# Linear attention and an erf-gated MLP in split fp32: order of the gates' forms, of the product's chunks, and of the gates' halves

## The chip, the cores and the metric

The kernel runs on one core of a Trainium2 chip. The metric is the device time of one execution in microseconds, as the median of three runs. The profile is of one further execution. Engines are named as in the profile: PE is TensorE (PEld its weight loads), DVE is VectorE, ACT is ScalarE, SP is SyncE, which here only issues DMAs, and POOL is GpSimd.

## The reference

A linear attention (8 batches, 8 heads, 576 tokens, head size 64) is normalised per head and feeds a gated MLP over all 4608 tokens:

```
kv  = einsum('bhsd,bhse->bhde', k, v)
o   = einsum('bhsd,bhde->bhse', q, kv)
x   = o / sqrt(mean(o*o, -1) + 1e-6) * g_norm      # to (4608, 512)
h   = x @ w_in                                     # 512 -> 2048
g   = h * erf(softplus(h))
out = g @ w_out                                    # 2048 -> 512
```

## The kernel before

The tokens are worked on in nine tiles of 512. T = 0 to 7 hold the first 512 tokens of each batch; T = 8 (which the code calls B) collects the last 64 of all eight. The MLP's 2048 hidden features are cut into 16 blocks of 128, and four blocks make a batch (BATCH = 4), so a tile has four batches b = 0 to 3.

The order of the instructions on every engine is written by hand (manual_schedule): each engine runs its own instructions in program order, and the framework adds the semaphores for data and buffers. Buffers come from pools that rotate. The eight PSUM banks are two for attention (ps_at), and six that `product` rotates through, two to each product, so a product can start when what the third product before it left in the same banks has been read.

Tiles T = 0 and 1 are done first, with plain fp32 matmuls (lines 592 and 471), while the weights are read and split. From T = 2 on (after 268 us) all MLP matmuls are in a split form. Every operand exists in three forms: form 0, high (rounded on ScalarE by a scaled copy, `upper`, line 385), form 1, low (the rest, VectorE, line 388), and form 2, both (a combination, VectorE, line 389). `thirds` makes all three. The weights' forms wait in DRAM and are loaded tile by tile: w_in_parts for a hidden block, w_out_parts for an output block, 768 KB each. w_out_parts has seven buffers.

`product` multiplies two operands in forms: n_ps takes the sums of forms 0 and 1 over four chunks k (8 matmuls), m_ps the sum of form 2 (4 matmuls). For a hidden block the chunks are four groups of 128 of the 512 inputs, so chunk p of x_forms comes from head pair p. For an output row block j (128 of the tile's tokens) the chunks are the four feature blocks of the batch, each with its own w_out_parts tile.

The main loop runs over m, which counts batches across tiles; T and b belong to the hidden side of m, and the result side lags by one batch. One turn of the loop is:

- four hidden products, i = 0 to 3. After each, ScalarE copies n_ps, scaled, to h (line 717), VectorE adds m_ps (line 419, called `add`), and ScalarE takes softplus into s (line 719). At i = 0 and i = 1 the gates of the batch before, old_h, are cut into their three forms, one half of the tokens each (g_forms0, g_forms1), by `cut`.
- erf of s on ScalarE, in two instructions, with a table load ahead (line 724).
- four result products, j = 0 to 3, each added to the accumulator e by VectorE (line 665 or 414 for n_ps, line 419 for m_ps). With the last batch of a tile each j is followed by the store of its rows. After j = 1 VectorE multiplies h by s (line 735).
- between these, at numbered places, the pieces of attention for head pair b of the next tile: key-value products and transposes (lines 279 to 301), apply (306, 307), mean (328 to 342), norm (348, 351, 360) and split, which cuts the normalised x into x_forms. For the last tile T = 8, which is prepared during T = 7, the attention outputs already lie in x_last, and only square, mean, norm and split are left.
- loads of weights, put on SP's queue by `fetch` at fixed places.

After the last hidden batch (m = batches - 1) a final turn (m = batches) has results only; `g_next` hands it the half that was cut early.

The two lines that place the cut in the loop are:

```
            if len(g) <= i < 2:
                g.append(cut(old_h, i))
```

Of the kernel before, what the change touches and what calls it, by code (L numbers as in the profile page):

```python
# [43 lines left out]
AF = mybir.ActivationFunctionType  # L44
ALU = mybir.AluOpType
# [13 lines left out]
def kernel(  # L59
# [10 lines left out]
    nc = tc.nc  # L70
    P = 128
# [33 lines left out]
    def softplus_table():  # L105
        nc.scalar.preload_act_table_set("softplus")  # L106
# [34 lines left out]
    for i in range(2):  # L141
        nc.gpsimd.dma_start(
            out=g_col[i * D : i * D + D, :], in_=g_norm.rearrange("(d one) -> d one", one=1)
# [100 lines left out]
    def weights():  # L244

        w_next("split")
        w_next("join")
        w_next("load")
# [134 lines left out]
    def upper(x, high):  # L383

        nc.scalar.activation(high, x, AF.Copy, scale=1.0 + 2.0**-13)  # L385

    def lower(x, high, low, both):
        nc.vector.tensor_tensor(out=low, in0=x, in1=high.bitcast(FP32), op=ALU.subtract)  # L388
        nc.vector.scalar_tensor_tensor(  # L389
            out=both,  # L390
            in0=low.bitcast(FP32),
            scalar=SHIFT,
            in1=high.bitcast(FP32),
            op0=ALU.mult,
            op1=ALU.add,
        )

    def thirds(x, high, low, both):
        upper(x, high)
        lower(x, high, low, both)  # L400
# [17 lines left out]
    def add(out_, ps):  # L418
        nc.vector.tensor_tensor(out=out_, in0=ps, in1=out_, op=ALU.add)  # L419
# [3 lines left out]
    def product(weights, moving):  # L423

        n_ps, m_ps = (
            pool.tile([P, G], FP32, name=name, tag=tag)
            for name, (pool, tag) in zip(("n_ps", "m_ps"), banks[:2])
        )
        banks.extend(banks[:2])
        del banks[:2]  # L430
        for ps, forms in ((n_ps, (0, 1)), (m_ps, (2,))):
            for form in forms:
                for k in range(4):
                    nc.tensor.matmul(  # L434
                        ps,
                        lhsT=weights(form, k),
                        rhs=moving(form, k),
                        start=(form == forms[0] and k == 0),
                        stop=(form == forms[-1] and k == 3),
                    )  # L440
        return n_ps, m_ps
# [57 lines left out]
    def unit(name):  # L499
        return gate.tile([P, G], FP32, name=name, tag=name[0])  # L500
# [30 lines left out]
    first_batch, batches = FIRST * NB, NG * NB  # L531
# [6 lines left out]
    def load_parts(which, n):  # L538

        pool = w_in_p if which == "in" else w_out_p  # L540
        for _ in range(n):
            if w_seq[which]:
                key = w_seq[which].pop(0)
                t = pool.tile([P, 3, G], FP32, name=f"w_{which}_parts", tag="w")
                nc.sync.dma_start(out=t, in_=w_kept[key])
                w_now.setdefault(key, []).append(t)
# [22 lines left out]
    for n in range(FIRST * FC + 1):  # L569
# [16 lines left out]
        done = n - LAG + 1  # L586
        if 0 <= done < whole:
            nc.vector.tensor_tensor(out=hs[done], in0=hs[done], in1=ss[done], op=ALU.mult)
        if T < FIRST:
# [9 lines left out]
            if n == whole:  # L599
                old_h = wide.tile([P, BATCH, G], FP32, name="h", tag="h")  # L600
            h = hs[n] = old_h[:, n - whole] if n >= whole else unit("h_sb")
            s = ss[n] = unit("s_sb")
# [43 lines left out]
    def hidden(T, f):  # L646

        w = w_now["in", f].pop(0).rearrange("p i (c f) -> p i c f", c=KC).bitcast(FP32R)
        return product(lambda form, c: w[:, form, c], lambda form, c: x_forms[T][:, form, c])

    def cut(h, half):

        t = late_r.tile([P, 3, BATCH, 2 * P], FP32R, name=f"g_forms{half}")
        thirds(h[:, :, half * 2 * P : half * 2 * P + 2 * P], *(t[:, i] for i in range(3)))
        return t

    def result(T, b, j, g, w):

        ps = product(
            lambda form, f: g[j // 2][:, form, f, j % 2 * P : j % 2 * P + P],  # L660
            lambda form, f: w[f][:, form],
        )
        if b == 0:
            es[j] = acc.tile([P, DM], FP32, name="e", tag="e")
            nc.vector.tensor_scalar(
                out=es[j], in0=ps[0], scalar1=SHIFT - 1.0, scalar2=None, op0=ALU.mult
            )
        else:
            add_scaled(es[j], ps[0], SHIFT - 1.0)
        add(es[j], ps[1])  # L670
        if b == NB - 1:
            store(T, j, es.pop(j))
# [4 lines left out]
    g_next = []  # L677
    for m in range(first_batch, batches + 1):
        T, b = divmod(m, NB)
        todo = []  # L680
        if T + 1 < NG:
            todo = list(attention(T + 1, b))
            if b == 0:
                side = late_r if T % 2 == FIRST % 2 else late
                x_forms[T + 1] = side.tile([P, 3, KC, G], FP32R, name=f"x_forms{(T + 1) % 2}")

        def piece():
            if todo:
                todo.pop(0)()

        places = (0, 2, 3, 5, 7, 8)
        if T + 1 == B:
            places = (0, 0, 0, 5, 7, 7)
        elif T + 2 == B and b == NB - 1:
            places = (0, 2, 3, 5, 7, 7)

        def pieces(place):
            while todo and places[-len(todo)] <= place:
                todo.pop(0)()

        def fetch(place):
            for which in FETCH[place].split():
                load_parts(which, 1)

        pieces(0)
        g, g_next = g_next, []
        if m < batches:
            h = wide.tile([P, BATCH, G], FP32, name="h", tag="h")
            s = gate_r.tile([P, BATCH, G], FP32, name="s", tag="s")
        for i in range(BATCH):  # L710
            if m < batches:
                n_ps, m_ps = hidden(T, b * BATCH + i)
            fetch(i)
            if len(g) <= i < 2:
                g.append(cut(old_h, i))
            if m < batches:
                nc.scalar.activation(h[:, i], n_ps, AF.Copy, scale=SHIFT - 1.0)  # L717
                add(h[:, i], m_ps)
                nc.scalar.activation(s[:, i], h[:, i], AF.Softplus)  # L719
            pieces(i + 1)  # L720
        if m < batches:
            for i in range(2):
                part = s[:, 2 * i : 2 * i + 2]
                nc.scalar.activation(part, part, AF.Erf)  # L724
            if len(todo) < 3:
                softplus_table()
        T2, b2 = divmod(m - 1, NB)
        w = [w_now["out", b2 * BATCH + f].pop(0).bitcast(FP32R) for f in range(BATCH)]
        for j in range(J):
            result(T2, b2, j, g, w)  # L730
            fetch(BATCH + j)
            if j == 1 and m < batches:
                for i in range(2):
                    part = slice(2 * i, 2 * i + 2)
                    nc.vector.tensor_tensor(  # L735
                        out=h[:, part], in0=h[:, part], in1=s[:, part], op=ALU.mult
                    )
            if j == 2 and m == batches - 1:

                g_next.append(cut(h, 0))  # L740
            pieces(BATCH + 1 + j)
        old_h = h

# [32 lines left out]
```

## Time and profile before

| | |
|---|---|
| time, median of three runs | 981.02 us (979.07 to 981.49) |
| profiled execution | 979.31 us, span on the core 977.5 us, mean granted clock 0.997 |
| n_ps matmuls in `product`, 128x512 | 896 (hidden) and 928 (results) |
| m_ps matmuls in `product`, 128x512 | 448 and 464 |
| upper form of half the gates (ScalarE, 128x1024) | 58 times, 1055 ns |
| low form, both form of it (VectorE) | 58 times each, 1222 and 1225 ns |
| product of h and s (VectorE, 128x1024) | 56 times, 1218 ns |
| copy n_ps to h, softplus (ScalarE, 128x512) | 112 times each, 584 and 634 ns |

Busy shares and waits in the profile are to be read with one thing in mind: matmuls are pipelined, so each lasts about 0.39 us in the records but the next one starts 0.227 us after it. A product's twelve matmuls start within 2.72 us. A line of the timeline gives the start in us from the beginning of the span, the duration in us, the engine, the line and operation, the tiles written and read, and the count of instructions merged into it; in brackets stands the idle time ahead of it and who ended it.

### The profile page before, as it was taken

To read this page: it belongs to the slowest core of one execution; us is meant where nothing else is said; L and a number is where in the kernel's file an instruction comes from. 1 tells how busy PE (TensorE), PEld (TensorE's weight loads), DVE (VectorE), ACT (ScalarE), POOL (GpSimd) and SP (SyncE) were. 2 spreads that over 40 slices of the span, in tenths; PEclk is the share of its full clock that TensorE was granted. 3 is DMA by queue.
4 is the path that set the end of the run, shared out by engine and by line. 5 is a ranking of instruction groups with operands and counts; after the bars stand their busy time and mean duration, and the time that the engine had idled before them with its cause. 6 is when DMAs were issued, how large, how long until landed. Compare 5 with 4: busy or idle time off the path is not lost.

```text
span 977.5 us, 11728 instructions
## 1 busy us (share of the span) xinstructions
PE 944.5 (97%) x4328; PEld 677.0 (69%) x4328; DVE 728.8 (75%) x1031; ACT 615.9 (63%) x821; POOL 2.4 (0%) x10
## 2 busy tenths in 40 slices
PE   6899999999999999999999999999999999989997
PEld 4344444444478877787878777878787777768885
DVE  3987857865377777777777877777888777777666
ACT  4888765676666666666666666666666666665550
POOL 0000000000000000000000000000000000000000
PEclk9999999999999999999999999999999999999998
DMA  9865408879199886998599869987786669757952
GB/s 282 244 204 173 151 1 317 310 305 374 45 349 360 315 293 222 336 364 291 190 314 372 298 220 288 366 301 266 246 347 247 252 219 374 272 203 274 372 197 75
DMA packets 100936, 259.76 MB, mean 266 GB/s; under 512 B 44048, under 2 KB 57360, under 8 KB 100880
## 3 DMA queue, kind: packets, MB, share of 16 engines
q1 hardware_dynamic: 99248, 256.73, 73.7%
q10 hardware_dynamic: 1568, 2.29, 0.8%
q8 instruction: 34, 0.56, 0.2%
q14 instruction: 22, 0.18, 0.1%
q0 software_dynamic: 64, 0.00, 0.0%
HBM read 224.40 MB, written 34.60 MB: 265 GB/s over the span
## 4 chain that ended last, share of the span: by engine, by line
PE 75%; DVE 13%; ACT 7%; DMA 2%; issue 2%; SPq 0%; DVEq 0%
PE n_ps L434 33%; PE m_ps L434 17%; PE o_ps L471 9%; PE h_ps L592 8%; PE se_ps L307 3%; DVE h L735 3%; DVE e L419 2%; PE qt_ps L301 2%; PE kv_ps L279 1%; DVE x L360 1%; DVE h L419 1%; ACT s L719 1%; ACT s L724 1%; DVE e L414 1%; DMA v_sb<-in_v_dram 1%
## 5 line engine op out<-in xcount | busy, mean ns | idle before, releaser
L434 PE MATMUL n_ps<-x_forms,w_in_parts 128*128 128x512 f32 x896 | 233.0, 402 | 4.5 <-ACT x_forms L385 4.1
L434 PE MATMUL n_ps<-w_out_parts,g_forms 128*128 128x512 f32 x928 | 233.2, 393 | 4.0 <-DMA w_out_parts<-w_out 3.8
L434 PEld LDWEIGHTS n_ps<-w_out_parts,g_forms 128*128 128x128 f32 x928 | 174.4, 188 | 44.2 <-DMA w_out_parts<-w_out 5.1
L434 PEld LDWEIGHTS n_ps<-x_forms,w_in_parts 128*128 128x128 f32 x896 | 166.6, 188 | 48.3 <-issue 9.6
L719 ACT ACTIVATE s<-h 128x512 f32<-128x512 f32 x112 | 71.0, 634 | 203.7 <-DVE h L419 203.7
L434 PE MATMUL m_ps<-w_out_parts,g_forms 128*128 128x512 f32 x464 | 125.3, 392 | 1.1 <-DVE h L419 1.1
L434 PE MATMUL m_ps<-x_forms,w_in_parts 128*128 128x512 f32 x448 | 120.1, 390 | 0.0
L592 PE MATMUL h_ps<-xT,w_in_sb 128*128 128x512 f32 x256 | 115.0, 593 | 2.9 <-DVE xT L360 2.0
L419 DVE TENSOR_TENSOR h<-m_ps,h 128x512 f32<-128x512 f32 x112 | 77.0, 688 | 52.5 <-ACT h L717 49.7
L388 DVE TENSOR_TENSOR g_forms<-h,g_forms 128x1024 fp32r<-128x1024 f32 x58 | 70.9, 1222 | 46.9 <-ACT g_forms L385 46.6
L434 PEld LDWEIGHTS m_ps<-w_out_parts,g_forms 128*128 128x128 f32 x464 | 87.5, 189 | 20.2 <-DVE h L419 1.9
L471 PE MATMUL o_ps<-w_out_sb,h_sb 128*128 128x512 f32 x224 | 100.6, 592 | 0.0
L434 PEld LDWEIGHTS m_ps<-x_forms,w_in_parts 128*128 128x128 f32 x448 | 84.1, 188 | 17.7
L419 DVE TENSOR_TENSOR e<-m_ps,e 128x512 f32<-128x512 f32 x116 | 80.2, 692 | 16.7 <-PE m_ps L434 8.1
L592 PEld LDWEIGHTS h_ps<-xT,w_in_sb 128*128 128x128 f32 x256 | 48.4, 190 | 63.2 <-issue 56.9
L414 DVE SCALAR_TENSOR_TENSOR e<-n_ps,e 128x512 f32<-128x512 f32 x88 | 60.2, 684 | 24.6 <-PE n_ps L434 24.6
L471 PEld LDWEIGHTS o_ps<-w_out_sb,h_sb 128*128 128x128 f32 x224 | 42.1, 190 | 49.8 <-issue 48.0
L717 ACT ACTIVATE h<-n_ps 128x512 f32<-128x512 f32 x112 | 65.5, 584 | 15.0 <-PE n_ps L434 14.9
L389 DVE SCALAR_TENSOR_TENSOR g_forms<-g_forms 128x1024 fp32r<-128x1024 f32 x58 | 71.1, 1225 | 2.0
L735 DVE TENSOR_TENSOR h<-h,s 128x1024 f32<-128x1024 f32 x56 | 65.9, 1218 | 1.1 <-ACT s L724 1.1
L385 ACT ACTIVATE g_forms<-h 128x1024 fp32r<-128x1024 f32 x58 | 61.2, 1055 | 7.2 <-DVE h L735 5.7
L106 ACT ACT_TABLE_LOAD x44 | 56.5, 1283 | 0.8
(84 smaller groups left out, 940.4 us busy)
## 6 DMA issues: line engine op xcount, KB each, us to landing
w_out_parts<-w_out SPq DMA_DIRECT2D x116, 768.0 KB, 7.6
w_in_parts<-w_in SPq DMA_DIRECT2D x112, 768.0 KB, 6.3
w_in<-w_new SPq DMA_DIRECT2D x16, 768.0 KB, 5.6
w_out<-w_new SPq DMA_DIRECT2D x16, 768.0 KB, 6.5
k_sb<-in_k_dram SPq DMA_DIRECT2D x29, 288.0 KB, 5.6
v_sb<-in_v_dram SPq DMA_DIRECT2D x29, 288.0 KB, 5.5
q_sb<-in_q_dram SPq DMA_DIRECT2D x32, 256.0 KB, 5.4
w_raw<-in_moe_w_out_dram SPq DMA_DIRECT2D x8, 1024.0 KB, 5.1
```

The lines of the kernel that those rows point to most:

```text
L106: nc.scalar.preload_act_table_set("softplus")
L385: nc.scalar.activation(high, x, AF.Copy, scale=1.0 + 2.0**-13)
L388: nc.vector.tensor_tensor(out=low, in0=x, in1=high.bitcast(FP32), op=ALU.subtract)
L389: nc.vector.scalar_tensor_tensor(out=both, in0=low.bitcast(FP32), scalar=SHIFT, in1=high.bitcast(FP32), op0=ALU.mult, op1=ALU.add,)
L414: nc.vector.scalar_tensor_tensor(out=out_, in0=ps, scalar=scale, in1=out_, op0=ALU.mult, op1=ALU.add)
L419: nc.vector.tensor_tensor(out=out_, in0=ps, in1=out_, op=ALU.add)
L434: nc.tensor.matmul(ps, lhsT=weights(form, k), rhs=moving(form, k), start=(form == forms[0] and k == 0), stop=(form == forms[-1] and k == 3),)
L471: nc.tensor.matmul(o_ps[j], lhsT=g[:, j * P : j * P + P], rhs=w_out_sb[:, f, :], start=(f == 0), stop=last,)
L592: nc.tensor.matmul(h_ps, lhsT=w_in_sb[:, c, f * P : f * P + P], rhs=xT[T][:, c, :], start=(c == 0), stop=(c == KC - 1),)
L717: nc.scalar.activation(h[:, i], n_ps, AF.Copy, scale=SHIFT - 1.0)
L719: nc.scalar.activation(s[:, i], h[:, i], AF.Softplus)
L735: nc.vector.tensor_tensor(out=h[:, part], in0=h[:, part], in1=s[:, part], op=ALU.mult)
```

## The change

Four things are changed.

- In `product`, n_ps is summed chunk by chunk, forms 0 and 1 of each, instead of form 0 over all chunks and then form 1.
- The cut of the gates is parted into `cut_upper` (ScalarE) and `cut_lower` (VectorE). In each turn both halves' upper forms are issued at i = 0, ahead of the copy of n_ps to h; VectorE's parts stay at i = 0 and i = 1.
- Erf, and the product of h and s, still run as two instructions each, but a half is now two of the four 128-token groups in all four feature blocks, not two feature blocks with all tokens.
- In the turn of the last hidden batch, the product of half 0 is made after j = 0, followed by its upper form; its lower forms and the product of half 1 come after j = 1. Before, both products came after j = 1 and the cut of half 0 after j = 2.

```
-            for form in forms:
-                for k in range(4):
+            for k in range(4):
+                for form in forms:
                     nc.tensor.matmul(
...
-    def cut(h, half):
+    def part(h, half):
+        return h[:, :, half * 2 * P : half * 2 * P + 2 * P]
+
+    def cut_upper(h, half):
 
         t = late_r.tile([P, 3, BATCH, 2 * P], FP32R, name=f"g_forms{half}")
-        thirds(h[:, :, half * 2 * P : half * 2 * P + 2 * P], *(t[:, i] for i in range(3)))
+        upper(part(h, half), t[:, 0])
         return t
+
+    def cut_lower(h, half, t):
+        lower(part(h, half), *(t[:, i] for i in range(3)))
...
-        g, g_next = g_next, []
+        g, done = g_next, len(g_next)
+        g_next = []
...
-            if len(g) <= i < 2:
-                g.append(cut(old_h, i))
+            if i == 0:
+                for half in range(done, 2):
+                    g.append(cut_upper(old_h, half))
+            if done <= i < 2:
+                cut_lower(old_h, i, g[i])
...
             for i in range(2):
-                part = s[:, 2 * i : 2 * i + 2]
-                nc.scalar.activation(part, part, AF.Erf)
+                nc.scalar.activation(part(s, i), part(s, i), AF.Erf)
...
-            if j == 1 and m < batches:
-                for i in range(2):
-                    part = slice(2 * i, 2 * i + 2)
-                    nc.vector.tensor_tensor(
-                        out=h[:, part], in0=h[:, part], in1=s[:, part], op=ALU.mult
-                    )
-            if j == 2 and m == batches - 1:
-
-                g_next.append(cut(h, 0))
+            if j == 1 and m == batches - 1:
+                cut_lower(h, 0, g_next[0])
+
+            for half in range(2) if j == 1 and m < batches - 1 else (j,) if j < 2 and m == batches - 1 else ():
+                nc.vector.tensor_tensor(
+                    out=part(h, half), in0=part(h, half), in1=part(s, half), op=ALU.mult
+                )
+            if j == 0 and m == batches - 1:
+                g_next.append(cut_upper(h, 0))
```

## The prediction

> **What bounds the kernel now.** I read the page's busy shares first, then who waited for whom on TensorE, then the timeline at each place where TensorE waits. The page:
>
> ```profile
> PE 944.5 (97%) x4328; PEld 677.0 (69%) x4328; DVE 728.8 (75%) x1031; ACT 615.9 (63%) x821; POOL 2.4 (0%) x10
> ```
>
> TensorE sets the time, so only its holes can be won. The function `product` exists from 268 us on. TensorE's waits from 275 us on:
>
> ```profile
> PE n_ps L434 <- ACT x_forms L385: 4.1, 2, 3.0
> PE n_ps L434 <- DMA w_out_parts<-w_out: 3.8, 2, 2.7
> PE qt_ps L301 <- DVE x L360: 2.7, 10, 0.3
> PE m_ps L434 <- DVE h L419: 1.1, 2, 0.5
> ```
>
> The third line belongs to the tiles T = 2 to 6: qt_ps waits for the normalised x. There VectorE runs without a gap from the add of j = 1 (614.32) through the two products of h and s to x (620.03). The other waits all lie after 770 us. The timeline at these places (start, duration, engine, line, operation, count, idle time before and its releaser):
>
> ```profile
> 770.67 0.84 PE L434 MATMUL n_ps<-x_forms,w_in_parts 128*128 128x512 f32 x3
> 772.61 1.42 PE L434 MATMUL n_ps<-x_forms,w_in_parts 128*128 128x512 f32 x5 [1.10 <-ACT x_forms L385]
> ...
> 805.59 0.84 PE L434 MATMUL n_ps<-w_out_parts,g_forms 128*128 128x512 f32 x3
> 807.58 1.43 PE L434 MATMUL n_ps<-w_out_parts,g_forms 128*128 128x512 f32 x5 [1.15 <-DMA w_out_parts<-w_out]
> ...
> 866.93 0.84 PE L434 MATMUL n_ps<-x_forms,w_in_parts 128*128 128x512 f32 x3
> 870.79 1.43 PE L434 MATMUL n_ps<-x_forms,w_in_parts 128*128 128x512 f32 x5 [3.03 <-ACT x_forms L385]
> ...
> 957.40 0.84 PE L434 MATMUL n_ps<-w_out_parts,g_forms 128*128 128x512 f32 x3
> 960.92 1.75 PE L434 MATMUL n_ps<-w_out_parts,g_forms 128*128 128x512 f32 x5 [2.68 <-DMA w_out_parts<-w_out]
> 962.47 1.91 PE L434 MATMUL m_ps<-w_out_parts,g_forms 128*128 128x512 f32 x4
> ```
>
> Each wait falls after three matmuls: the fourth reads chunk 3, which comes last. After 960.92 the matmuls are also slow: four take 1.71 us to the next product at 964.18, where they elsewhere take 0.91. The last view is the chain behind the waits of tile T = 7, in its fourth batch:
>
> ```profile
> 851.36 0.68 DVE L419 TENSOR_TENSOR h<-m_ps,h 128x512 f32<-128x512 f32 x1
> 852.08 0.64 ACT L719 ACTIVATE s<-h 128x512 f32<-128x512 f32 x1 [3.92 <-DVE h L419]
> 852.62 1.04 ACT L385 ACTIVATE g_forms<-h 128x1024 fp32r<-128x1024 f32 x1
> 853.57 0.58 ACT L717 ACTIVATE h<-n_ps 128x512 f32<-128x512 f32 x1
> 853.69 1.22 DVE L388 TENSOR_TENSOR g_forms<-h,g_forms 128x1024 fp32r<-128x1024 f32 x1 [1.65 <-ACT g_forms L385]
> 856.09 0.68 DVE L419 TENSOR_TENSOR h<-m_ps,h 128x512 f32<-128x512 f32 x1
> 856.83 1.20 PE L434 MATMUL m_ps<-w_out_parts,g_forms 128*128 128x512 f32 x4 [0.53 <-DVE h L419]
> ```
>
> ScalarE idles 3.92 us, then does softplus and the second half's upper form, and only then can VectorE cut that half: VectorE stands 1.65 us, and TensorE waits for the next add. The norm's first step (L348) starts at 769.70, 794.24, 818.78, 843.34 and 867.87 in this tile, every 24.54 us. One turn of the chain is: norm, x_forms, cut, adds, softplus, erf, Ln/Exp/Square, norm. TensorE alone needs less: its batch from 770.67 to 794.71 took 24.04, of which 1.26 was the wait, so 22.78. Hence in T = 7 the chain over ScalarE and VectorE sets the pace; in T = 2 to 6 attention's extra matmuls make TensorE's batch 25.2 us and hide it.
>
> [...] the second upper form, whose input h was ready since about 842, runs only behind softplus at 852.62. [...] the slow stretch after 960.92 lasts about 3.7 us (961.6 to 965.3) at 0.43 instead of 0.227 us per matmul, but its idle time was only 2.8 us, and the 3.0 us at 866.93 brought no slow stretch. [...] L388 reads h in strides of token halves in 1222 ns, L735 reads contiguous h and s in 1218.
>
> **The change, part by part.** The counts of matmuls, activations, vector operations and DMAs stay; SP's and POOL's orders do not move, and nothing passes a DMA.
>
> (a) Both upper forms ahead of the h copy at i = 0. The second one (1.05 us) moves into ScalarE's idle time (2.7 to 3.9 us) before softplus. Queued behind it is the h copy of i = 0, some 1.0 us later; the add that waits for it stands behind the cut of half 0 on VectorE (370.07 upper, 371.43 copy, 374.54 add in T = 3), so 1.5 us or more of slack is left. It also now waits for result j = 3 to have read the old g_forms1, but in the attention batches it starts at least 2 us after that, and elsewhere inside the first product's 1.98 us. What it removes: from the add of i = 0 to the cut of half 1 was 853.69 - 851.36 = 2.33; now VectorE follows itself, as from 848.36 to 848.97, 0.61. So 1.72 us leave each turn: 24.54 - 1.72 = 22.82, which matches TensorE's 22.78.
>
> In T = 2 to 6 this is worth nothing: VectorE is only done with the adds earlier, and the chain to qt_ps starts at TensorE's own j = 1. In T = 7, TensorE's losses by products are: 829.66, 0.81 us more than its 1.81; 846.91 to 854.19, 0.49 + 0.29 + 0.83. These 2.4 us go. At 866.93 the loss was 3.18. Now L348 follows the end of j = 1's m_ps by about 4.4 (0.04 to its add, then VectorE's own spacing 0.61 + 2.27 + 0.78 + 0.61, as from 614.32 to 618.59), x_forms' low form ends 3.6 later (0.71 + 0.73 + 0.79 + 0.67 + 0.69 from the rows 769.70 to 772.59), at 8.0 to 8.3. T = 8's first product starts at 5.43 (two products of 2.72) and wants low at 5.43 + 7 x 0.227 = 7.02. A loss of 1.0 to 1.3 remains, 1.9 to 2.2 go.
>
> (b) Products by chunk first. A wait for chunk 3 now comes after six matmuls: 3 x 0.227 = 0.68 us move in front of it. For x_forms it gives less, since the next matmul wants the low form, which ends 0.67 + 0.69 after the upper starts: at 770.67 the eighth may start at 773.33, against 773.64 (0.31). In (a)'s sum at 866.93 it is contained. At 805.59 the loss was 1.31. The two loads are issued at 800.67, behind the store at 799.98, which waits for e of j = 3, on the chain; that comes 0.7 earlier, the data thus at about 806.85 instead of 807.58; the seventh matmul then wants it at 805.3 + 1.36 = 806.66. About 0.2 remain, 1.1 go. At 957.40 the load starts when result j = 3 first reads for m_ps (956.9) and takes 3.96; that order is not changed, so 0.68 go.
>
> (c) Halves of tokens for erf and the gates' product: same element counts, no new instruction, 0 +- 0.3 us. In the last batch the product of half 0 and its cut come earlier: low of half 0 is ready by about 955.6 and both by 956.9, before TensorE's 957.4; half 1 is cut by about 963.2, some 0.5 later than now, and is wanted after 964. I count 0.
>
> (d) The slow clock at the end cost 0.42 + 0.80 + 0.52 = 1.74 us. The idle time before it falls from 2.84 to 2.16 us. The trace shows no threshold: 1.3 us idle gave none, 2.84 did. Bounds 0 and 1.74; I take 1.74[...].
>
> Sum in the profiled span: 0.31 + 1.1 + 2.4 + 2.05 + 0.68 = 6.5, and 1.74 = 8.3: 977.5 - 8.3 = 969.2. That execution took 979.31; the three timed runs have a median of 981.02 (979.07 to 981.49). Off the median: 972.7.
>
> **The rivals.** First: chain right, clock not regained (or lost at another gap[...]): -6.5, 974.5. For it: the idle time stays above 2 us. Second: weight transfers take over T = 7 as batches shrink by 1.7 us; then (a)'s 4.5 return as DMA waits like that at 805.59: about 978. Against it: T = 8 does its batches in 21.76 us (8 loads of 768 KB each as well) without a wait until the last. Third, slower: alternating forms cost TensorE time per matmul, for the moving operand jumps 8 KB instead of 2 KB. 1824 n_ps matmuls are touched; from 8.3 / 1824 = 4.5 ns each it decides; at 8 ns it is +6.3, 987. Against it: results already step through separate w_out tiles at the same 0.227. Fourth: the tokens' halves or the order change nothing that TensorE sees, 981; against it stands the 24.54 of four turns, equal to the summed chain.
>
> **How the numbers follow.** Chances: forecast 0.50, clock kept slow 0.30, transfers 0.11, slower 0.05, nothing 0.04. A measurement of this kernel can tell about 0.3% from no change, here 2.9 us, 978.1. Faster: 0.80 and 0.07 of the transfers' case, 0.87; same: 0.04 + 0.04 = 0.08; slower 0.05. The range goes from 970.0 (both sums high, and the low one of the three runs) to 977.5 (part of the transfers' case).
>
> **What would show it.** Right: n_ps waits in groups x6 instead of x3; L348 every 22.8 us in T = 7; no VectorE wait for g_forms' upper of 1.65 us; m_ps never waiting for h L419; the matmuls after the last wait at 0.227 us. Wrong: n_ps above 0.227 per matmul in T = 2 to 6; new waits for w_in_parts or w_out_parts between 795 and 865; T = 7's batches still 24 us.

## The result, and the profile after

The changed kernel takes 972.71 us, the median of four runs (972.46 to 974.32), against 980.74 of the kernel before in four runs (979.07 to 981.49). The ratio is 0.9924, with a 95% interval of 0.9907 to 0.9941: 0.8% faster. The profiled execution, one of the four, took 972.92 us, with a span of 971.1.

The page of the changed kernel, its line of busy shares:

```profile
PE 944.2 (97%) x4328; PEld 677.5 (70%) x4328; DVE 728.4 (75%) x1031; ACT 615.2 (63%) x821; POOL 2.4 (0%) x10
```

Each engine's work is what it was, within 0.7 us; the span lost holes, not work. TensorE's waits from 275 us on (total us, times, longest):

```profile
PE qt_ps L301 <- DVE x L360: 2.7, 10, 0.3
PE n_ps L434 <- DMA w_out_parts<-w_out: 2.5, 2, 2.1
PE n_ps L434 <- ACT x_forms L385: 1.2, 2, 0.8
PE n_ps L434 <- DVE x_forms L388: 0.5, 2, 0.2
```

The first line, which belongs to T = 2 to 6, has not moved. The wait for ScalarE's x_forms fell from 4.1 to 1.2 us, the one for the adds (m_ps, line 419) is gone. The low form, L388, is new on the list: by chunk, it is wanted one matmul after the high one. The same places in the timeline:

```profile
772.08 1.52 PE L434 MATMUL n_ps<-x_forms,w_in_parts 128*128 128x512 f32 x6
774.02 0.49 PE L434 MATMUL n_ps<-x_forms,w_in_parts 128*128 128x512 f32 x1 [0.42 <-ACT x_forms L385]
774.75 0.50 PE L434 MATMUL n_ps<-x_forms,w_in_parts 128*128 128x512 f32 x1 [0.23 <-DVE x_forms L388]
...
806.82 1.52 PE L434 MATMUL n_ps<-w_out_parts,g_forms 128*128 128x512 f32 x6
808.81 0.73 PE L434 MATMUL n_ps<-w_out_parts,g_forms 128*128 128x512 f32 x2 [0.47 <-DMA w_out_parts<-w_out]
...
864.62 1.52 PE L434 MATMUL n_ps<-x_forms,w_in_parts 128*128 128x512 f32 x6
866.92 0.49 PE L434 MATMUL n_ps<-x_forms,w_in_parts 128*128 128x512 f32 x1 [0.77 <-ACT x_forms L385]
...
953.24 1.52 PE L434 MATMUL n_ps<-w_out_parts,g_forms 128*128 128x512 f32 x6
956.82 0.72 PE L434 MATMUL n_ps<-w_out_parts,g_forms 128*128 128x512 f32 x2 [2.06 <-DMA w_out_parts<-w_out]
957.38 1.09 PE L434 MATMUL m_ps<-w_out_parts,g_forms 128*128 128x512 f32 x4
```

Six matmuls now run ahead of each wait, and the four after the last wait reach the next product (958.31) in 0.93 us. The chain in the fourth batch of T = 7, all engines:

```profile
844.48 2.00 ACT L385 ACTIVATE g_forms<-h 128x1024 fp32r<-128x1024 f32 x2
...
849.21 0.68 DVE L419 TENSOR_TENSOR h<-m_ps,h 128x512 f32<-128x512 f32 x1
849.81 1.22 DVE L388 TENSOR_TENSOR g_forms<-h,g_forms 128x1024 fp32r<-128x1024 f32 x1
849.93 0.63 ACT L729 ACTIVATE s<-h 128x512 f32<-128x512 f32 x1 [2.97 <-DVE h L419]
...
852.20 0.69 DVE L419 TENSOR_TENSOR h<-m_ps,h 128x512 f32<-128x512 f32 x1
```

Both upper forms are done by 846.5, so VectorE goes from the add to the second cut in 0.60 us, where it took 2.33. From add to add are 2.99 us, before 4.73. TensorE waits for none of these.

Where the time went is best counted from T = 7's first product on (770.67 before, 772.08 after), in stretches between the same matmuls:

| stretch | before, us | after, us | less |
|---|---|---|---|
| first product of T = 7 | 4.12 | 3.94 | 0.18 |
| to the wait for weights in the second batch | 30.80 | 30.80 | 0 |
| the product with that wait, to j = 1 | 4.62 | 3.95 | 0.67 |
| to the first product of T = 8 | 56.72 | 53.85 | 2.87 |
| first product of T = 8 | 6.04 | 4.29 | 1.75 |
| to the first product of the last turn | 84.43 | 84.33 | 0.10 |
| to the end | 20.10 | 17.86 | 2.24 |

Together 7.8 us. This execution was 1.4 us late at the start of T = 7; that delay stood already at T = 2 (third product at 276.24 instead of 274.71), behind code that the change doesn't touch. It comes from the clock: from 34.73 to 38.14 us TensorE was granted half of it (0.50; in the kernel before 1.00 over the same stretch), and the matmuls, 0.3 us late ahead of this, are 2.0 us late behind it. In four of the ten profiles of this case the clock is at half near 35 us, and their first product comes at 269.5 to 270.7 us; in the other six it comes at 268.2 to 268.6.

### The profile page after: what moved, and what is told of

Its sections match the earlier page's. It is cut to its first block, busy times and chain, and to the rows that moved or that the text cites. A ratio compares the mean times of both kernels' runs of the same rounds, so it can differ in the third digit from the quotient of the medians.

```text
span 971.1 us, 11732 instructions
## 1 busy us (share of the span) xinstructions
PE 944.2 (97%) x4328; PEld 677.5 (70%) x4328; DVE 728.4 (75%) x1031; ACT 615.2 (63%) x821; POOL 2.4 (0%) x10
## 4 chain that ended last, share of the span: by engine, by line
PE 81%; DVE 12%; ACT 4%; DMA 2%; issue 1%; SPq 0%; DVEq 0%
PE n_ps L434 35%; PE m_ps L434 18%; PE h_ps L592 10%; PE o_ps L471 9%; PE se_ps L307 3%; DVE h L745 3%; DVE e L419 2%; PE qt_ps L301 2%; PE kv_ps L279 2%; DMA w_out_parts<-w_out 1%; DVE x L360 1%; DVE e L414 1%; DVE u L351 1%; DVE u L348 1%; PE ms_ps L328 1%
## 5 line engine op out<-in xcount | busy, mean ns | idle before, releaser
L388 DVE TENSOR_TENSOR g_forms<-h,g_forms 128x1024 fp32r<-128x1024 f32 x58 | 70.6, 1218 | 1.5 <-ACT g_forms L385 1.2
L385 ACT ACTIVATE g_forms<-h 128x1024 fp32r<-128x1024 f32 x58 | 58.9, 1059 | 13.8 <-PE m_ps L434 11.0
L385 ACT ACTIVATE x_forms<-x 128x512 fp32r<-128x512 f32 x28 | 17.7, 631 | 66.8 <-DVE x L360 66.8
```

## The experiments

My theory: the order on ScalarE shortens the chain that paces T = 7; the chunk order moves three matmuls ahead of a wait; and shorter idle time keeps the clock. The rivals are in each expectation. The kernel before ran beside them: median 980.72 us with the first four, 980.85 with the last four. The changed kernel itself was not run again, so differences from it are from its 972.71.

**Only the upper forms first.** Old kernel, with

```
+            if i == 0:
+                for half in range(done, 2):
+                    g.append(cut_upper(old_h, half))
+            if done <= i < 2:
+                cut_lower(old_h, i, g[i])
```

> The old kernel with one part of the change: both upper forms of the gates at i = 0, ahead of the copy of n_ps. Products by form first, halves as before. My theory (the chain over ScalarE and VectorE set the pace in T = 7, and 1.7 us leave each of its turns): T = 7's waits on VectorE go and the wait at the start of T = 8 shrinks by about 1.7 us; L348 every 22.7 to 22.8 us there; 2.9 + 1.7 = 4.6 us less than before, about 976. The wait for the last weight tile and the slow clock after it stay. Rival (the products' chunk order brought the gain, ScalarE's order none): within 0.5 us of before, L348 still every 24.5.

Measured: 974.98 us (972.46 to 975.98), ratio 0.9935 (0.9922 to 0.9947), 5.7 us less than before. L348 in T = 7 starts at 771.89, 795.93, 819.16, 841.96 and 864.78: the last two turns take 22.80 and 22.82. TensorE's losses at products in T = 7 (0.81, 0.49, 0.29, 0.83) are all gone, and the one at the start of T = 8 fell from 3.18 to 1.62. So ScalarE's order did it, and both the rival here and the prediction's fourth, that TensorE sees nothing of the change, are out. The wait for weights in T = 7 was shorter too, 0.45 instead of 1.31, which I had not put into this part. The end kept its slow clock, five matmuls took 2.14 us, to m_ps at 959.75:

```profile
957.61 2.34 PE L434 MATMUL n_ps<-w_out_parts,g_forms 128*128 128x512 f32 x5 [2.58 <-DMA w_out_parts<-w_out]
```

**Only the chunk order.** Old kernel, with

```
-            for form in forms:
-                for k in range(4):
+            for k in range(4):
+                for form in forms:
```

> The old kernel with one part of the change: products by chunk first. My theory: 0.2 us at each of the two waits for x_forms, 0.7 at the wait for weights in T = 7, 2.2 to 2.4 at the last wait with the clock kept: 3.3 us less, about 977.4; T = 7's turns stay at 24.5 us. If the clock is lost all the same, 1.6 us less, 979. Rival (alternating forms cost time in every matmul): longer than before, and batches of T = 2 to 6 longer than 25.2 us.

Measured: 979.24 us (977.21 to 981.34 in 21 runs), ratio 0.9988 (0.9981 to 0.9995): 1.5 us less, not 3.3. Alternating forms costs nothing in T = 2 to 6: n_ps keeps its 1.81 us for eight matmuls, and the time from T = 2's first product to T = 7's is 502.1 us, before 502.2. T = 7's turns stay at 24.53 to 24.56. At the last wait the clock was kept in the profiled execution (1.99 us idle), as I had it. But it was lost at another place, the start of T = 8, where the profile of the kernel before has it kept:

```profile
871.67 1.52 PE L434 MATMUL n_ps<-x_forms,w_in_parts 128*128 128x512 f32 x2 [2.36 <-ACT x_forms L385]
872.98 1.91 PE L434 MATMUL m_ps<-x_forms,w_in_parts 128*128 128x512 f32 x4
874.69 3.61 PE L434 MATMUL n_ps<-x_forms,w_in_parts 128*128 128x512 f32 x8
```

Eight matmuls take 3.41 us to the next start instead of 1.81, and four 1.71 instead of 0.91: 2.4 us lost after an idle time of 2.36.

**Without the halves of tokens.** Changed kernel, with erf and the gates' product by pairs of feature blocks, and in the last hidden batch both products after j = 1 and the whole cut of half 0 after j = 2:

```
-                nc.scalar.activation(part(s, i), part(s, i), AF.Erf)
+                half_s = s[:, 2 * i : 2 * i + 2]
+                nc.scalar.activation(half_s, half_s, AF.Erf)
```

> The changed kernel without its third part: erf and the gates' product by pairs of feature blocks again, and in the last hidden batch the products after j = 1 and the whole cut of half 0 after j = 2. My theory: that part lies beside TensorE's work everywhere, so within 0.5 us of the changed kernel, about 972.7; TensorE's waits the same. Rival (the earlier low form of half 0 is what keeps the last products going, since by chunk they want it at the second matmul): a new wait of TensorE for g_forms in the last turn and 1 us or more longer.

Measured: 973.18 us (971.97 to 974.09), ratio 0.9919 (0.9905 to 0.9932), 0.5 from the changed kernel and inside the range of its runs. TensorE's waits are those of the changed kernel (w_out_parts 2.6, x_forms 1.2 and 0.5 us) and none is for g_forms. The third part is worth nothing that these runs can see. Yet in its profiled execution the clock was lost after the last wait, with 2.25 us idle: eight matmuls in 3.33 us to the next start.

```profile
957.49 3.49 PE L434 MATMUL n_ps<-w_out_parts,g_forms 128*128 128x512 f32 x8
```

**One product by form first again.** Changed kernel, with form first for j = 0 of the last turn alone:

```
+            order = [(k, form) for k in range(4) for form in forms]
+            if form_first:
+                order.sort(key=lambda kf: kf[1])
```

> The changed kernel, with one product of all (j = 0 of the last turn) summed by form first again, so that TensorE idles some 2.7 to 2.8 us ahead of the last weight tile instead of 2.1. Theory that the shorter idle time kept the clock: 0.7 us of matmuls and 1.7 us of slow clock come back, 2.4 us more than the changed kernel, about 975.1, with matmuls at 0.43 us after the wait. Rival [...]: 0.7 us more, about 973.4, matmuls at 0.227.

Measured: 974.70 us (973.27 to 976.38), ratio 0.9934 (0.9922 to 0.9947), 2.0 more than the changed kernel. The profile shows three matmuls, an idle time of 3.08 us, and the slow clock:

```profile
955.25 2.32 PE L437 MATMUL n_ps<-w_out_parts,g_forms 128*128 128x512 f32 x5 [3.08 <-DMA w_out_parts<-w_out]
957.37 1.79 PE L437 MATMUL m_ps<-w_out_parts,g_forms 128*128 128x512 f32 x4
```

From 955.25 to 959.00, nine matmuls took 3.75 us, 1.7 more than 9 x 0.227, as the theory had it. It does not rule out chance: the ranges of the two kernels' runs overlap, one profile is one case, and other profiles lost the clock after 2.25 us (without the halves) and kept it after 2.54 (gates' product earlier). In the profiles of the last section both count, the length of the idle time and how it falls on the times, whole multiples of 3.41 us apart, at which the granted clock changes.

**The last load in a free buffer.** Changed kernel, with

```
+                if which == "out" and not w_seq["out"]:
+                    pool = w_in_p
```

> The changed kernel, with the very last weight tile loaded into a buffer of w_in_parts that nobody needs any more, so that the load needn't wait for the result j = 3 before it. Theory (that wait is the only one at the end, and the slow clock comes from idle time of about 2 us or more): the wait of 2.1 us goes, and with it the slow clock that some executions have there; 2.1 to 2.8 us less than the changed kernel, 970.2, no matmuls at 0.43 us after 950. Rival (the transfer itself is late, because the queue is busy with earlier loads): within 0.5 us of the changed kernel.

Measured: 970.31 us (969.09 to 971.14), ratio 0.9894 (0.9879 to 0.9909), 2.4 us less than the changed kernel. The products follow each other every 2.72 us from 946.34 to 959.93, through the whole last turn and without a wait. So the last tile had come late because its load waited for a buffer, not because the transfer queued behind others.

**The gates' product one place earlier.** The profile still had TensorE waiting for qt_ps in T = 2 to 6, where I had said that the change is worth nothing. With it erf ends earlier there, too, so the product of h and s may go ahead of result j = 1 on VectorE. Changed kernel, with

```
-            for half in range(2) if j == 1 and m < batches - 1 else (j,) ...
+            for half in range(2) if j == (T + 1 >= B) and m < batches - 1 else (j,) ...
```

> The changed kernel, with the product of h and s of T = 2 to 6 after j = 0 instead of j = 1 on VectorE. Theory: there TensorE waits 0.2 to 0.4 us in each batch (kv_ps, qt_ps) for the norm, whose start VectorE sets by the products ahead of it; the change's ScalarE order lets erf end 1.6 us earlier, in time for this place. Norm 0.9 us earlier, the waits go, batches 24.9 instead of 25.2 us, 20 of them: 6 us less than the changed kernel, about 966.5. Rival (ScalarE's Square or erf comes last there): norm not earlier, batches at 25.2, the same time as the changed kernel.

Measured: 964.98 us (964.53 to 969.17), ratio 0.9850 (0.9829 to 0.9871), 7.7 us less than the changed kernel. First the changed kernel's product and norm in one batch of T = 5, then those of this one:

```profile
612.56 2.01 ACT L733 ACTIVATE s<-s 128x1024 f32<-128x1024 f32 x2
616.36 2.35 DVE L745 TENSOR_TENSOR h<-h,s 128x1024 f32<-128x1024 f32 x2
620.02 0.68 DVE L348 SCALAR_TENSOR_TENSOR u<-ms_ps,u 128x512 f32<-128x512 f32 x1
```

```profile
608.69 2.01 ACT L733 ACTIVATE s<-s 128x1024 f32<-128x1024 f32 x2
609.79 2.36 DVE L745 TENSOR_TENSOR h<-h,s 128x1024 f32<-128x1024 f32 x2 [0.41 <-ACT s L733]
615.21 0.68 DVE L348 SCALAR_TENSOR_TENSOR u<-ms_ps,u 128x512 f32<-128x512 f32 x1
```

From erf's start to the norm it was 7.46 us, now 6.52, so the norm is 0.94 earlier. The wait for qt_ps on VectorE is gone from TensorE's list up to 778 us, and so are the 5.9 us that the weight loads for qt_ps waited; from batch to batch it is 24.85 and 24.95 us in turn instead of about 25.2. The weight loads' 6.7 us for kv_ps stay, now put down to issue, so VectorE had not set that wait. The sum of what the profile shows: T = 2 to 6 are 5.6 us shorter (496.5 instead of 502.1 from the first product to T = 7's first), that first product of T = 7 loses 0.9 less, and the product that waited for weights in T = 7 0.7 less, while the wait at the end is 0.5 longer: 6.7 in all; the two profiled spans differ by 6.6. The median's further 1.1 us no profile shows. They fit the clock: the profiled execution (966.29 us, granted clock 0.997) has the slow stretch near 35 us, while three of the five runs have 0.999 and take 964.5 to 965.0 us.

**The same move in the old kernel.** The edit `j == (T + 1 >= B)`, with the old cut:

> The old kernel (old cut, old orders) with the same move of the gates' product in T = 2 to 6 to after j = 0. Theory: with the old cut erf ends 1.6 us later, VectorE stands before the product, and the norm starts 0.5 us later than before instead of 0.9 earlier; each batch of T = 2 to 6 grows by up to 0.5 us: between 981 and 990. Rival (erf's end doesn't matter): 6 us less than before, as in the changed kernel.

Measured: 990.45 us (989.52 to 990.83), ratio 1.0099 (1.0084 to 1.0113): 9.6 us more than before, at the upper end of what was expected. VectorE stands before the product in 19 batches, 30.9 us in all:

```profile
618.97 2.36 DVE L735 TENSOR_TENSOR h<-h,s 128x1024 f32<-128x1024 f32 x2 [1.68 <-ACT s L724]
```

The next batch's product comes at 644.66, 25.69 us later. In the profile T = 2 to 6 are 8.1 us longer than before, out of 10.2; most of the rest lies at the start of T = 8, where this execution lost the clock. One edit, 7.7 us of gain with the new cut and 9.6 of loss with the old one: the new order on ScalarE makes erf earlier in T = 2 to 6 as well (in T = 5 it starts 2.94 us after the product of j = 0, with the old order 4.68), but nothing that TensorE waits for used it.

**Both together.** The edits of the free buffer and of the earlier product:

> The changed kernel with both edits of the two runs ahead of it: the last weight tile in a free buffer, and the gates' product of T = 2 to 6 after j = 0. They lie at different places, so they should add: 8 to 9 us less than the changed kernel, about 964.3.

Measured: 963.07 us (962.40 to 963.30), ratio 0.9820 (0.9806 to 0.9833), 9.6 us less than the changed kernel, where 8 to 9 were expected; the parts' 2.4 and 7.7 make 10.1. It is the fastest here, 1.8% ahead of the kernel before.

## Why the prediction was right

Forecast 972.7, measured 972.71; that they agree so closely is partly luck, as the terms show.

(a) The chain was right, in mechanism and size. 4.45 us were forecast (2.4 in T = 7 and 2.05 at T = 8), the profile has 2.87 + 1.75 = 4.62, so the two errors nearly cancel. L348's turns, forecast at 22.82, take 23.85, 23.41, 22.80 and 22.82. The first two are longer because TensorE, late from its own waits at 774 and 808, sets them: with the gates' product earlier, where the wait at 808 is gone, the second turn takes 22.79. This part alone gave 5.7 us in the medians, the wait for weights included; with the chunk order's 1.5 that makes 7.2 of the whole change's 8.0.

(b) Chunk first: for x_forms 0.18 instead of 0.31. For the weights in T = 7 the step "that comes 0.7 earlier, the data thus at about 806.85" failed in its size: 0.67 instead of 1.1 us. The two loads were issued 5.42 us ahead of the product instead of 4.92, but the data still let the waiting matmul start 1.99 us after the product, as before. Over the kernels that wait at this product the same figure lies between 1.13 (only the upper forms) and 2.57 (only the chunk order), so the landing has a spread of its own. What sets it, other transfers or the issue, stays open. At the last wait the order of events was as forecast.

(c) The halves: forecast 0 +- 0.3, measured within 0.5.

(d) The clock: "I take 1.74" came out in the profiled execution, which has 2.24 of the forecast 0.68 + 1.74. It was my estimate, which no measurement supported, and that it came out is luck. The step also left out the 3.03 us at 866.93, quoted further up, that had brought no slow clock. And the slow stretch that the prediction reads as 3.7 us from the matmuls is 3.41 in the record of the clock (961.82 to 965.24). What decides in these profiles is how much of the idle time falls into one window of 3.41 us, as the table of the last section shows; the changed kernel's 2.06 us happened to be split into 1.56 and 0.50. In its four runs the granted clock was 0.998, 0.998, 0.999 and, in the slowest one (974.32 us), 0.995, so this term is a chance per execution. In the profile the chunk order's 1.5 us instead of 3.3 is this term, lost at another gap, which the first rival had named; the granted clock of its 21 runs (median 0.996, before 0.997) does not show it regained either.

The slower rival, alternating forms, is out: in T = 2 to 6 n_ps keeps 1.81 us per eight matmuls. The transfers' rival too (by the prediction's own terms its time is 972.7 + 4.5 = 977.2, not 978): T = 7's last two turns shrank to 22.8 us and no new wait for weights came.

## What to carry to other kernels

ScalarE ran in the written order here: the second upper form, whose input h was done at 841.41, ran at 852.62 behind softplus, although ScalarE had idled for 3.92 us ahead of that. When an engine that works so stands between two of another engine's steps, look for work further down its queue that is already ready, and put it into the idle time ahead of the step that others wait for: 1.05 us moved on ScalarE took 1.7 us from each turn of the chain. Time won off TensorE's path is not nothing: ask what it makes possible (here the product one place earlier, 7.7 us more, which without it cost 9.6). And when a tile waits for a buffer, look for one that another stream has stopped using.

## What was not expected of the hardware

Whether TensorE falls to half clock is not told by the length of the idle time alone: it kept the full clock after 3.03 us (the kernel before, start of T = 8) and lost it after 2.25 us (without the halves, end). The trace records the clock that TensorE was granted. In the profiles of this case it is 1.00 or 0.50, and the times at which it changes lie whole multiples of 3.41 us apart: 961.82, 965.24 and 975.48 us in the kernel before (1 and 3 such steps), 34.73, 38.14 and 969.98 in the changed kernel (1 and 273), 38.48, 871.34 and 878.16 with the chunk order alone (244 and 2, so its slow stretch at the start of T = 8 lasts two steps). The 3.41 us from one such time to the next are called a window here. A window did not have to be idle throughout: TensorE was busy for 1.36 us (without the halves) and 1.39 us (only the chunk order) in windows that half clock followed. What counts in these profiles is how much of the idle time falls into one window. The kernel before at the start of T = 8, and the kernel without the halves at the end (each line: the window, its length, busy us and count of PE, PEld, DVE, ACT and POOL, the granted clock, the DMA share, GB/s):

```profile
866.25:869.66 3.41, 1.52 (x7) 0.94 (x5) 2.72 (x5) 2.81 (x4) 0.00 (x0) 1.00 0.65 195
869.66:873.08 3.42, 2.29 (x10) 1.92 (x11) 2.59 (x5) 2.18 (x3) 0.00 (x0) 1.00 0.09 36
...
953.88:957.29 3.41, 1.36 (x6) 1.16 (x7) 3.27 (x5) 0.00 (x0) 0.00 (x0) 1.00 0.29 119
957.29:960.71 3.42, 3.42 (x10) 2.64 (x9) 1.24 (x2) 0.00 (x0) 0.00 (x0) 0.50 0.23 61
```

In the first the 3.03 us are split into 1.90 and 1.13 and the clock stays; in the second 2.05 of the 2.25 us lie in one window and the next one runs at half clock. All idle times of TensorE of about 2 us and more from T = 2 to the last product, by the part that lies in one window:

| kernel and place | idle, us | most in one window, us | clock in the next window |
|---|---|---|---|
| only the chunk order, end | 1.99 | 1.10 | 1.00 |
| gates' product earlier, end | 2.54 | 1.39 | 1.00 |
| changed kernel, end | 2.06 | 1.56 | 1.00 |
| before, start of T = 8 | 3.03 | 1.90 | 1.00 |
| only the chunk order, start of T = 8 | 2.36 | 2.02 | 0.50 |
| without the halves, end | 2.25 | 2.05 | 0.50 |
| before, end | 2.68 | 2.51 | 0.50 |
| only the upper forms, end | 2.58 | 2.58 | 0.50 |
| old kernel, product earlier, end | 3.10 | 2.78 | 0.50 |
| old kernel, product earlier, start of T = 8 | 3.06 | 2.88 | 0.50 |
| one product by form first, end | 3.08 | 3.08 | 0.50 |

In these eleven cases up to 1.90 us in one window left the clock at 1.00, and 2.02 us and more brought 0.50. It is less sharp in the part ahead of T = 2, with fp32 matmuls, where a window with 1.83 us of idle time was followed by half clock and one with 1.97 was not; the changed kernel's (31.32 to 34.73 us) had 1.98 and was. Taking 2.0 us as the limit and windows of 3.41 us, an idle time of 2.68 us (before, end) should lose the clock in about six of ten executions, if its start falls anywhere in a window alike, and one of 2.06 (changed kernel) in about four. That is an estimate from these figures; no run tests it. By it, a shorter idle time makes the slow clock rarer. With the last load in a free buffer no idle time is left in the last turn, and in its profile the products there keep following each other every 2.72 us.
